# Second attention layer: one 1024-column feature map for two results, sums and evictions issued a product later, query weights cast on POOL

## The chip, the core and the metric

The program runs on one core of one Trainium2 chip. The core has a matrix engine (PE, with its weight loads listed as PEld), a vector engine (DVE), an activation engine (ACT), a general engine (POOL) and DMA queues, here all filled from SP. Each engine works through its own instructions in program order and waits on semaphores for the others. The metric is the device time of one execution in microseconds; lower is better.

## The reference

Four blocks follow each other: attention, feed-forward, attention, feed-forward. Both attention blocks use the same weights, and so do both feed-forward blocks. S is 2048, D is 1024, F is 3584, 32 heads of 32.

```python
phi = lambda t: jnp.where(t > 0, t + 1, jnp.exp(t)) + 1e-6
# attention: q, k, v = layernorm(x) @ wqkv, by heads
pq, pk = phi(q), phi(k)
kv = einsum("bhsd,bhse->bhde", pk, v);  z = sum over s of pk
o = (pq @ kv) / (pq . z + 1e-6);        x = x + o @ wo
# feed-forward: n = layernorm(x)
x = x + ((n @ w_gate) * (n @ w_up)) @ w_down
```

Attention is linear: keys and values of all 2048 rows are first folded into `kv` and `z`, then the queries are run through them.

## The kernel before

`X` holds all 16 row tiles (128 x 1024) on chip. The layers are numbered 0 (attention), 1 (feed-forward), 2 (attention), 3 (feed-forward). The order of work on every engine is the order of the Python calls: loops call a step of matmuls and then whatever small dictionaries (`plan`, filled by `at(step, function, ...)`) have noted for that step. Buffers come from three first-in first-out lists: `banks` (8 PSUM banks of 128 x 512 float32), `temps` (12 tiles of the same size in SBUF) and `slots` (17 tiles of 8 KB per partition). A buffer is put back at the point of the program at which its last use is issued; the next owner waits for that use by semaphore.

Layer 2's keys and values are computed in `kv_seven` (L465) in half precision by a seven-product scheme on 2 x 2 blocks. A group `g` is four row tiles; a unit `u` (8 in all) is one half of it, two row tiles, both for 1024 key columns (k) and 1024 value columns (v). A unit has 14 products of 4 matmuls each (L539), in the order of `SEQ` (L490): "1k 5k 1v 6k 2k 6v 7k 5v 7v 2v 4k 3k 4v 3v". Five PSUM banks carry it: `ak` takes 1k, 6k, 7k, 4k one on top of the other, `av` the same for v, `ck` takes 5k and later 3k, `cv` 5v and 3v, and `b` takes 2k on top of a copy of 1k and then 2v. Because the products pile up in one bank, each intermediate sum is read out between two products: ACT copies (L523, L544), DVE adds (L526). The other three banks hold the running `kv` sums.

Keys go through `phi` (L270): ACT computes an exponential (L277), DVE takes a minimum and adds (L278), DVE adds max(0, x) (L280). This is done four times per unit, for the results of 2k, 7k, 4k and 3k, each 128 x 512. Two of them read PSUM, two read an SBUF tile in which DVE has added two parts. Values are added by DVE straight into `vbs`, and 4v is copied there by ACT (L576). After unit u the matmuls `kp` (L497) fold the two row tiles of unit u-1 into `kv`.

Between the products, `plan` puts other work of the same engines: layernorm of row tiles 8 to 15 (statistics on DVE L220 and L223, inverse deviation on ACT L228 and L229, a small DVE product L231, the normalised tile on ACT L237, a transposing DMA L260), the block differences `x_sum` of the next group (DVE L212), and the cast of the two query weight slots (ACT L177, eight pieces of 128 x 1024). At step 92 both halves of the output weights are loaded.

Ahead of it, `down_seven` (layer 1) has 98 steps of 4 matmuls (L1146), whose own `plan` casts the key and value weights and forms their block sums. Earlier still, in the second pass of layer 1, `scale_begin(2)` and `scale_end(2)` work out the power-of-two scales of the attention weights: `scale_begin` runs ahead of quad 0 and `scale_end` (L359) ahead of quad 1 of that pass (a quad is 56 matmuls on L909). `scale_end` issues transposes on PE (L366), a chain of small DVE instructions (L368 to L383), and in their midst one ACT instruction (L381) that takes the logarithm of the scales `scw` into `lns2`, a bias of the exponentials on L277. ACT's next instructions are the copies of quad 1 (L920).

Of the kernel before, what the change touches and what calls it, by code (L numbers as in the profile page):

```python
# [35 lines left out]
def kernel(  # L36
# [128 lines left out]
    while D % FMAX:  # L165
        FMAX //= 2
    NST = D // FMAX

    ACOL = (1, 0, 2)
    xnTs = {}  # L170
# [4 lines left out]
    def cast_a(m, n, i):  # L175
        s = wA["kqv"[m]][n]
        nc.scalar.activation(out=h3(s, NB)[:, 2 * i:2 * i + 2, :], in_=v3(s, NB)[:, 2 * i:2 * i + 2, :],  # L177
                             func=ACT.Copy, scale=scw[:, 3 + m:4 + m])

    def w_blocks(which):  # L180
        a, b = (h3(s, NB) for s in wA[which])
# [30 lines left out]
        nc.vector.tensor_tensor(out=o, in0=x, in1=y, op=ALU.subtract)  # L212
    lns = {}

    def ln_stats(li, t, parts=tuple(range(NST))):
        if parts[0] == 0:
# [4 lines left out]
        if parts[-1] == NST - 1:  # L221
            mv = lns[(li, t)] = small.tile([P, 2], F32, tag="mv", name="mv")
            nc.vector.bn_aggr(out=mv[:], in_=st[:])  # L223

    def ln_rstd(li, t):
        mv = lns[(li, t)]
# [133 lines left out]
    def scale_end(m):  # L360
        n = NSC[m]
        q, t, qb = qsum.pop(m)
        b = banks.get()
        pt = b[:].bitcast(BF16)[:, 0:3 * P].rearrange("p (m n) -> p m n", n=P)
        for i in range(n):
            nc.tensor.transpose(out=pt[:, i, :], in_=qb[:, i, :], identity=ident[:])  # L366
        temps.put(t)
        nc.vector.tensor_reduce(out=q[:, 0:n], in_=pt[:, 0:n, :], axis=AX.X, op=ALU.add)  # L368
        banks.put(b)
        e = bexp[:, CSC[m]:CSC[m] + n]  # L370
        ei = e.bitcast(I32)
# [6 lines left out]
        nc.vector.tensor_scalar(out=sc, in0=sc, scalar1=AS if m == 2 else WS, scalar2=None, op0=ALU.mult)  # L378
        if m == 2:
            nc.vector.tensor_scalar(out=kaps[:], in0=e, scalar1=1.0 / AS, scalar2=None, op0=ALU.mult)  # L380
            nc.scalar.activation(out=lns2[:], in_=sc[:, 0:2], func=ACT.Ln)  # L381
# [84 lines left out]
    def kv_seven(kvp):  # L466
# [26 lines left out]
        def kp(t, first, last):  # L493
            u = t // TPG * 2 + t % 2
# [9 lines left out]
        def unit(u):  # L504
# [13 lines left out]
            def w4(a):  # L518
                return a[:].rearrange("p (c f) -> p c f", f=P)

            def copy(key, b):
                tm[key] = temps.get()
                nc.scalar.copy(out=tm[key][:], in_=b[:])  # L523

            def add(out, key, b):
                nc.vector.tensor_tensor(out=out, in0=w4(tm[key]) if len(out.shape) == 3 else tm[key][:],  # L526
                                        in1=w4(b) if len(out.shape) == 3 else b[:], op=ALU.add)

            for j, step in enumerate(SEQ.split()):
                i, w = int(step[0]), step[1]  # L530
                key = "b" if i == 2 else ("c" if i in (3, 5) else "a") + w
                if key not in bk:
                    bk[key] = banks.get()
                if i == 1 and w == "k":
                    bk["b"] = banks.get()
                b = bk[key]
                rhs = w_rhs(w, i)
                for k in range(KH):
                    nc.tensor.matmul(out=b[:], lhsT=lhs[i][:, k, pr * P:(pr + 1) * P], rhs=rhs[:, k, :],  # L539
                                     start=k == 0 and (i in (1, 5) or i == 2 and w == "v"), stop=k == KH - 1,  # L540
                                     skip_group_check=True)
                if i == 1:
                    if w == "k":
                        nc.scalar.copy(out=bk["b"][:], in_=b[:])  # L544
                    else:
                        copy("1v", b)
                elif i == 6:
                    copy("6" + w, b)
                elif i == 7:
                    copy("7" + w, b)  # L550
                    if w == "k":
                        add(tm["7k"][:], "7k", bk["ck"])
                        phi(tm["7k"], pk(1, 1), 0)
                    else:
                        add(vb(1, 1), "7v", bk["cv"])
                    temps.put(tm.pop("7" + w))
                elif i == 3:
                    if w == "k":
                        add(tm["6k"][:], "6k", b)
                        phi(tm["6k"], pk(1, 0), 0)  # L560
                    else:
                        add(vb(1, 0), "6v", b)
                    temps.put(tm.pop("6" + w))
                    banks.put(bk.pop(key))
                elif i == 2:
                    if w == "k":
                        phi(b, pk(0, 0), 0)
                    else:
                        add(vb(0, 0), "1v", b)
                        temps.put(tm.pop("1v"))  # L570
                        banks.put(bk.pop("b"))
                elif i == 4:
                    if w == "k":
                        phi(b, pk(0, 1), 0)
                    else:
                        nc.scalar.copy(out=vb(0, 1), in_=w4(b))  # L576
                    banks.put(bk.pop(key))
                for f, args in plan.get(u * 14 + j, ()):
                    f(*args)

        for u in range(2 * NG):
# [4 lines left out]
            if u % 2 == 1:  # L586
                slots.put(xgs.pop(u // 2))

        slots.put(*wA.pop("k"), *wA.pop("v"), wS.pop("k"), wS.pop("v"), wS.pop("d"))

        def rest():
            for t in tiles(2 * NG - 1):
# [446 lines left out]
    def down_seven(q, li, p, hs, wd, load_piece, cast_piece, ORDER, at, run, finish, xrow, nl, W2, final):  # L1039
# [43 lines left out]
        if not final:  # L1083
            if p == 0:
# [156 lines left out]
```

## Time and profile before

| | |
|---|---|
| median of 3 runs | 1521.29 us (1520.68 to 1521.84) |
| profiled execution | 1521.27 us, of which its span 1519.5 us; 1.8 us lie around the span |
| PE | 1495.6 us busy, 98% of the span |
| DVE, ACT, POOL | 987.5, 814.7, 89.6 us busy |
| mean granted PE clock | 0.997 |
| stretch of the 8 units of layer 2 (L539, first to the next stage's first matmul) | 764.98 to 886.03 us |
| PE idle in the span | 24 us |

The trace names stretches of the span by time. Layer 0 lies up to 250 us, layer 1 from 250 to 765 (its second pass from 504), layer 2 from 765 to 1000, layer 3 after it. A wait of PE is shown as the idle time before a matmul and the instruction that ended it; since matmuls overlap by some 0.16 us (379 ns each, one every 216 ns), a gap costs that much more than the idle time shown.

### The profile page before, as it was taken

How to read it: one execution, taken by the hardware profiler on the slowest of the kernel's cores; microseconds unless marked ns; L12 is line 12 of the kernel's file. 1: busy time of each engine (PE TensorE's matmuls, PEld its weight loads, DVE VectorE, ACT ScalarE, POOL GpSimd, SP SyncE). 2: the span in 40 equal slices, each digit the busy share in tenths (PEclk: the TensorE clock that was granted, in tenths of full speed). 3: DMA queues.
4: the chain of work that ended last, by engine and by line, in shares of the span. 5: the costliest groups of instructions: out<-in, count | busy, mean ns of one | idle time of the engine just before them, and what ended most of it. 6: DMA issues, size and time to landing. Idle time of an engine off the chain costs nothing.

```text
span 1519.5 us, 18411 instructions
## 1 busy us (share of the span) xinstructions
PE 1495.6 (98%) x7109; PEld 683.2 (45%) x7109; DVE 987.5 (65%) x1675; ACT 814.7 (54%) x1196; POOL 89.6 (6%) x46
## 2 busy tenths in 40 slices
PE   9999999999999899999997999999999999999999
PEld 4444444444444344444443444444444444444444
DVE  6667989988686566667866676864444853444452
ACT  4678875767667377764447576633334232333420
POOL 0000005971000000000000000000000000000000
PEclk9999999999999999999999999999999999999999
DMA  8696147564489778759421200464223578343513
GB/s 242 181 304 215 56 90 215 149 184 139 129 246 324 222 235 263 242 191 280 147 76 23 75 1 0 146 236 173 111 111 128 159 259 338 120 166 111 196 71 128
DMA packets 219655, 253.90 MB, mean 167 GB/s; under 512 B 68528, under 2 KB 195504, under 8 KB 208816
## 3 DMA queue, kind: packets, MB, share of 16 engines
q1 hardware_dynamic: 219568, 252.74, 52.4%
q8 instruction: 55, 0.90, 0.3%
q14 instruction: 32, 0.26, 0.1%
HBM read 196.08 MB, written 40.89 MB: 156 GB/s over the span
## 4 chain that ended last, share of the span: by engine, by line
PE 92%; DVE 4%; ACT 3%; DMA 1%; issue 0%; SPq 0%; DVEq 0%
PE b L909 44%; PE b L1146 22%; PE b L746 7%; PE b L609 7%; PE b L777 7%; PE b L539 2%; ACT f L277 1%; PE b L760 1%; DVE st L220 1%; DVE s L280 1%; ACT xn L237 1%; DMA s<-in_A_wqkv_dram 1%; PE b L628 0%; DVE f L526 0%; PE b L727 0%; DVE f L278 0%
## 5 line engine op out<-in xcount | busy, mean ns | idle before, releaser
L909 PE MATMUL b<-s,s 128*128 128x512 f16 x3136 | 680.4, 380 | 4.0 <-ACT b L920 4.0
L909 PEld LDWEIGHTS <-s 128*128 128x128 f16 x3136 | 307.1, 98 | 376.2 <-issue 7.6
L1146 PE MATMUL b<-s,s 128*128 128x512 f16 x1568 | 339.1, 379 | 0.0
L925 DVE TENSOR_TENSOR f<-f,b 128x512 f32<-128x512 f32 x232 | 159.3, 687 | 230.6 <-ACT f L914 216.3
L914 ACT COPY f<-b 128x512 f32<-128x512 f32 x284 | 165.9, 584 | 226.8 <-PE b L909 226.8
L1146 PEld LDWEIGHTS <-s 128*128 128x128 f16 x1568 | 153.3, 98 | 185.2
L920 ACT COPY b<-b 128x512 f32<-128x512 f32 x104 | 59.2, 570 | 127.3 <-PE b L909 127.3
L419 ACT ACTIVATE s<-s,scw 128x1024 f16<-128x1024 bf16 x112 | 122.7, 1151 | 2.0 <-DMA s<-in_B_w_gate_dram 1.8
L746 PE MATMUL b<-s,s 128*128 128x512 bf16 (+1 forms) x512 | 120.3, 379 | 0.0
L777 PE MATMUL b<-s,s 128*128 128x512 bf16 x512 | 118.5, 379 | 0.3 <-DVE s L769 0.3
L875 ACT ACTIVATE s<-s,scw 128x1792 f16<-128x1792 bf16 x48 | 83.0, 1783 | 61.6 <-DMA s<-in_B_w_down_dram 54.2
L539 PE MATMUL b<-s,s 128*128 128x512 f16 x448 | 101.6, 379 | 13.8 <-ACT f L523 5.1
L609 PE MATMUL b<-s,s 128*128 128x512 bf16 x512 | 112.1, 379 | 0.9 <-DMA s<-in_A_wqkv_dram 0.7
L830 POOL TENSOR_SCALAR s<-s,scw 128x1024 f16<-128x1024 bf16 x28 | 88.0, 3159 | 257.1 <-DVE X L779 243.9
L929 DVE SCALAR_TENSOR_TENSOR s<-f,b 128x512 f16<-128x512 f32 x108 | 74.2, 687 | 40.8 <-PE b L909 24.4
L929 DVE SCALAR_TENSOR_TENSOR s<-f,f 128x512 f16<-128x512 f32 x116 | 83.2, 717 | 4.0
L220 DVE BATCH_NORM_STATS2 st<-X 128x6 f32<-128x512 bf16 x128 | 82.3, 681 | 2.4 <-DMA X<-in_A_x_dram 2.4
L777 PEld LDWEIGHTS <-s 128*128 128x128 bf16 x512 | 50.0, 98 | 60.9 <-DVE s L769 1.0
L609 PEld LDWEIGHTS <-s 128*128 128x128 bf16 x512 | 49.6, 98 | 60.6 <-issue 1.2
L746 PEld LDWEIGHTS <-s 128*128 128x128 bf16 (+1 forms) x512 | 49.9, 98 | 59.4
L539 PEld LDWEIGHTS <-s 128*128 128x128 f16 x448 | 43.4, 97 | 69.3 <-issue 20.6
L1057 DVE TENSOR_TENSOR s<-s,s 128x1024 f16<-128x1024 f16 x80 | 52.9, 678 | 23.3 <-PE b L1146 23.3
(116 smaller groups left out, 1093.8 us busy)
## 6 DMA issues: line engine op xcount, KB each, us to landing
s<-wc SPq DMA_DIRECT2D x56, 1024.0 KB, 6.6
s<-dc SPq DMA_DIRECT2D x32, 896.0 KB, 5.6
wc<-s SPq DMA_DIRECT2D x28, 1024.0 KB, 5.1
s<-in_B_w_down_dram SPq DMA_DIRECT2D x24, 896.0 KB, 5.7
s<-in_A_wqkv_dram SPq DMA_DIRECT2D x17, 1024.0 KB, 7.9
s<-in_B_w_down_dram SPq DMA_DIRECT2D x14, 1024.0 KB, 7.8
s<-in_B_w_gate_dram SPq DMA_DIRECT2D x28, 512.0 KB, 6.7
s<-in_B_w_up_dram SPq DMA_DIRECT2D x28, 512.0 KB, 7.9
```

Source lines behind the costliest of these rows:

```text
L220: nc.vector.bn_stats(out=st[:, c, :], in_=X[:, t, c * FMAX:(c + 1) * FMAX])
L419: nc.scalar.activation(out=h, in_=v, func=ACT.Copy, scale=scw[:, m:m + 1])
L539: nc.tensor.matmul(out=b[:], lhsT=lhs[i][:, k, pr * P:(pr + 1) * P], rhs=rhs[:, k, :], start=k == 0 and (i in (1, 5) or i == 2 and w == "v ...
L609: nc.tensor.matmul(out=b[:], lhsT=xnT[:, k, tl * P:(tl + 1) * P], rhs=w[:, k, :], start=(k == 0), stop=(k == KD - 1))
L746: nc.tensor.matmul(out=b[:], lhsT=w[:, k, j * P:(j + 1) * P], rhs=xnT[:, k, :], start=(k == 0), stop=(k == KD - 1))
L777: nc.tensor.matmul(out=b[:], lhsT=v3(pqs[g], G)[:, c, tl * P:(tl + 1) * P], rhs=v3(M[n], NB)[:, c, :], start=(c == 0), stop=(c == KD - 1))
L830: nc.gpsimd.tensor_scalar(out=h3(s, D)[:, i, :], in0=v3(s, D)[:, i, :], scalar1=scw[:, 2:3], scalar2=None, op0=ALU.mult)
L909: nc.tensor.matmul(out=o[m][:], lhsT=W.get(j, m, st[i - 1], k), rhs=mv[i - 1][:, k, :], start=start and k == 0, stop=stop and k == KH - 1, ...
L914: nc.scalar.copy(out=d[m][:], in_=o[m][:])
L925: nc.vector.tensor_tensor(out=d[m][:], in0=d[m][:], in1=o[m][:], op=ALU.add)
L929: nc.vector.scalar_tensor_tensor(out=h3(hs[h], 2 * G)[:, pos, g * G:(g + 1) * G], in0=x[:], scalar=HS, in1=y[:], op0=ALU.mult, op1=ALU.mult)
L1146: nc.tensor.matmul(out=bank[(key, tl)][:], lhsT=lhs(i, j, tl), rhs=h3(wd[2 * pi + j // WPC], NB)[:, j % WPC, :], start=(j == 0 and i in (1 ...
```

## The change

The key path of a unit, the order of products, the place of some evictions and several pieces of planned work are different:

- The results of 7k and 3k stay in one 128 x 1024 float32 tile (`wide`, in a slot of its own, one half per unit parity). ACT copies 6k and 7k into its two halves, DVE adds `ck` to each half (`addw`), and one exponential, one minimum/add and one max/add of 1024 columns follow (`phi_exp`, `phi_end`).
- The add of 7k and the two DVE instructions of the wide map are issued one step later, the copy of 4v two steps later, that is after the first product of the next unit. 4k comes before 2v.
- The query weights are cast by POOL (`cast_q`) and loaded at steps 8 and 9. The second half of the output weights is loaded after the last unit.
- Of the layernorm work of tiles 8 to 15, the statistics of the second half of the columns are taken during `down_seven` of layer 1; three tiles use the DVE form of the normalisation (`ln_norm`), and the steps of all are others.
- The logarithm into `lns2` is no longer part of `scale_end`; it is at step 3 of `down_seven`.

```diff
+    def cast_q(n, i):
+        s = wA["q"][n]
+        nc.gpsimd.tensor_scalar(out=h3(s, NB)[:, 2 * i:2 * i + 2, :], in0=v3(s, NB)[:, 2 * i:2 * i + 2, :],
+                                scalar1=scw[:, 4:5], scalar2=None, op0=ALU.mult)
...
+    def last_part(li, t):
+        return 0 if li == 2 and t >= 2 * TPG else NST - 1
+
+    def ln_stats(li, t, parts=tuple(range(NST)), early=False):
+        if early:
+            if not st8:
+                st8.append(temps.get())
...
+    def phi_exp(b, c):
+        m = temps.get()
+        e = m[:].bitcast(BF16)[:, 0:b.shape[-1]]
+        nc.scalar.activation(out=e, in_=b, func=ACT.Exp, bias=lns2[:, c:c + 1], scale=kaps[:, c:c + 1])
+        return m, e
+
+    def phi_end(b, dst, c, m, e):
+        nc.vector.tensor_scalar(out=e, in0=e, scalar1=scw[:, 3 + c:4 + c], scalar2=epss[:, c:c + 1],
+                                op0=ALU.min, op1=ALU.add)
+        nc.vector.scalar_tensor_tensor(out=dst, in0=b, scalar=0.0, in1=e, op0=ALU.max, op1=ALU.add)
+        temps.put(m)
...
-            nc.scalar.activation(out=lns2[:], in_=sc[:, 0:2], func=ACT.Ln)
...
-        for t in range(2 * TPG, NT):
-            i = 4 + 9 * (t - 2 * TPG)
+        for t, i in zip(range(2 * TPG, NT), (3, 8, 17, 31, 36, 45, 59, 64)):
             at(i, ln_stats, 2, t, (0,))
-            at(i + 1, ln_stats, 2, t, (1,))
-            at(i + 3, ln_rstd, 2, t)
-            at(i + 5, ln_apply, 2, t)
-            at(i + 6, tr_tile, 2, t)
-        for g, i in ((1, 15), (2, 46), (3, 76)):
+            if i % 14 == 8:
+                at(i + 5, ln_norm, 2, t)
+                at(i + 6, tr_tile, 2, t)
+            else:
+                at(i + 4, ln_rstd, 2, t)
+                at(i + 6, ln_apply, 2, t)
+                at(i + 7, tr_tile, 2, t)
+        at(66, lambda: temps.put(st8.pop()))
+        for g, i in ((1, 19), (2, 45), (3, 75)):
             for j in range(4):
                 at(i + 2 * j, x_sum, g, j)
-        at(20, load_w, "q", 0)
-        at(21, load_w, "q", 1)
+        at(8, load_w, "q", 0)
+        at(9, load_w, "q", 1)
         for n in range(DC):
             for i in range(4):
-                at(31 + 11 * n + 2 * i, cast_a, 1, n, i)
-        at(92, lambda: wA.update(o=[load_cols(wo_v, n) for n in range(DC)]))
+                at(20 + 16 * n + 4 * i, cast_q, n, i)
+        at(90, lambda: wA.update(o=[load_cols(wo_v, 0)]))
...
-        SEQ = "1k 5k 1v 6k 2k 6v 7k 5v 7v 2v 4k 3k 4v 3v"
+        SEQ = "1k 5k 1v 6k 2k 6v 7k 5v 7v 4k 2v 3k 4v 3v"
+        wides = slots.get()
...
+            def addw(n, b):
+                v = wd2[:, n * NB:(n + 1) * NB]
+                nc.vector.tensor_tensor(out=v, in0=v, in1=b[:], op=ALU.add)
+
+            def out4(b):
+                nc.scalar.copy(out=vb(0, 1), in_=w4(b))
+                banks.put(b)
...
+                elif i in (6, 7) and w == "k":
+                    n = i - 6
+                    nc.scalar.copy(out=wd2[:, n * NB:(n + 1) * NB], in_=b[:])
+                    if i == 7:
+                        later(1, addw, 1, bk["ck"])
...
                 elif i == 3:
                     if w == "k":
-                        add(tm["6k"][:], "6k", b)
-                        phi(tm["6k"], pk(1, 0), 0)
+                        addw(0, b)
+                        later(1, phi_end, wd2, pkv[:, r0 + 1, :], 0, *phi_exp(wd2, 0))
...
                     else:
-                        nc.scalar.copy(out=vb(0, 1), in_=w4(b))
-                    banks.put(bk.pop(key))
-                for f, args in plan.get(u * 14 + j, ()):
+                        later(2, out4, bk.pop(key))
+                for f, args in plan.pop(u * 14 + j, ()):
                     f(*args)
...
+        wA["o"].append(load_cols(wo_v, 1))
...
+                at(3, lambda: nc.scalar.activation(out=lns2[:], in_=scw[:, 3:5], func=ACT.Ln))
+                for u in range(2 * TPG):
+                    at((57, 71)[u // TPG] + 3 * (u % TPG), ln_stats, 2, 2 * TPG + u, (NST - 1,), True)
```

More of the change, by code (lines that the diff above doesn't have):

```diff
@@ L167 @@
     NST = D // FMAX
+    st8 = []
     ACOL = (1, 0, 2)
@@ L213 @@
     lns = {}
-    def ln_stats(li, t, parts=tuple(range(NST))):
-        if parts[0] == 0:
+    def last_part(li, t):
[4 more added lines that the diff above has]
+                st8.append(temps.get())
+            u = 6 * NST * (t - 2 * TPG)
+            lns[(li, t)] = st8[0][:][:, u:u + 6 * NST].rearrange("p (c s) -> p c s", s=6)
+        elif (li, t) not in lns:
             lns[(li, t)] = small.tile([P, NST, 6], F32, tag="st", name="st")
@@ L220, in ln_stats @@
             nc.vector.bn_stats(out=st[:, c, :], in_=X[:, t, c * FMAX:(c + 1) * FMAX])
-        if parts[-1] == NST - 1:
+        if not early and len(parts) == NST or not early and parts[-1] == last_part(li, t):
             mv = lns[(li, t)] = small.tile([P, 2], F32, tag="mv", name="mv")
-            nc.vector.bn_aggr(out=mv[:], in_=st[:])
+            nc.vector.bn_aggr(out=mv[:], in_=st[:] if not isinstance(st, bass.AP) else st)
     def ln_rstd(li, t):
@@ L470, in at @@
             plan.setdefault(step, []).append((f, args))
[L472 to L473 removed]
+        for t, i in zip(range(2 * TPG, NT), (3, 8, 17, 31, 36, 45, 59, 64)):
             at(i, ln_stats, 2, t, (0,))
[L475 to L479 removed]
+            if i % 14 == 8:
[7 more added lines that the diff above has]
+        for g, i in ((1, 19), (2, 45), (3, 75)):
             for j in range(4):
                 at(i + 2 * j, x_sum, g, j)
[L482 to L483 removed]
+        at(8, load_w, "q", 0)
+        at(9, load_w, "q", 1)
         for n in range(DC):
             for i in range(4):
[L486 to L487 removed]
+                at(20 + 16 * n + 4 * i, cast_q, n, i)
+        at(90, lambda: wA.update(o=[load_cols(wo_v, 0)]))
         pks = slots.get()
         pkv = v3(pks, D)
[L491 removed]
+        SEQ = "1k 5k 1v 6k 2k 6v 7k 5v 7v 4k 2v 3k 4v 3v"
+        wides = slots.get()
+        wide = wides[:].bitcast(F32).rearrange("p (u n) -> p u n", n=D)
         def kp(t, first, last):
@@ L519, in w4, with later @@
                 return a[:].rearrange("p (c f) -> p c f", f=P)
+            wd2 = wide[:, u % 2]
+            def later(n, f, *args):
+                at(u * 14 + j + n, f, *args)
             def copy(key, b):
@@ L525, in add @@
             def add(out, key, b):
-                nc.vector.tensor_tensor(out=out, in0=w4(tm[key]) if len(out.shape) == 3 else tm[key][:],
-                                        in1=w4(b) if len(out.shape) == 3 else b[:], op=ALU.add)
+                nc.vector.tensor_tensor(out=out, in0=w4(tm[key]), in1=w4(b), op=ALU.add)
+                temps.put(tm.pop(key))
+            def addw(n, b):
[4 more added lines that the diff above has]
+                banks.put(b)
             for j, step in enumerate(SEQ.split()):
@@ L546, in unit @@
                         copy("1v", b)
+                elif i in (6, 7) and w == "k":
[3 more added lines that the diff above has]
+                        later(1, addw, 1, bk["ck"])
                 elif i == 6:
-                    copy("6" + w, b)
+                    copy("6v", b)
                 elif i == 7:
[L550 to L556, printed above, removed]
+                    copy("7v", b)
+                    add(vb(1, 1), "7v", bk["cv"])
                 elif i == 3:
                     if w == "k":
-                        add(tm["6k"][:], "6k", b)
-                        phi(tm["6k"], pk(1, 0), 0)
+                        addw(0, b)
+                        later(1, phi_end, wd2, pkv[:, r0 + 1, :], 0, *phi_exp(wd2, 0))
                     else:
                         add(vb(1, 0), "6v", b)
-                    temps.put(tm.pop("6" + w))
                     banks.put(bk.pop(key))
@@ L566, in unit @@
                     if w == "k":
-                        phi(b, pk(0, 0), 0)
+                        phi_end(b[:], pk(0, 0), 0, *phi_exp(b[:], 0))
                     else:
                         add(vb(0, 0), "1v", b)
-                        temps.put(tm.pop("1v"))
                         banks.put(bk.pop("b"))
@@ L573, in unit @@
                     if w == "k":
-                        phi(b, pk(0, 1), 0)
-                    else:
-                        nc.scalar.copy(out=vb(0, 1), in_=w4(b))
-                    banks.put(bk.pop(key))
-                for f, args in plan.get(u * 14 + j, ()):
+                        phi_end(b[:], pk(0, 1), 0, *phi_exp(b[:], 0))
+                        banks.put(bk.pop(key))
+                    else:
+                        later(2, out4, bk.pop(key))
+                for f, args in plan.pop(u * 14 + j, ()):
                     f(*args)
@@ L587, in kv_seven @@
                 slots.put(xgs.pop(u // 2))
-        slots.put(*wA.pop("k"), *wA.pop("v"), wS.pop("k"), wS.pop("v"), wS.pop("d"))
+        for i in sorted(plan):
+            for f, args in plan[i]:
+                f(*args)
+        slots.put(*wA.pop("k"), *wA.pop("v"), wS.pop("k"), wS.pop("v"), wS.pop("d"), wides)
+        wA["o"].append(load_cols(wo_v, 1))
         def rest():
```

## The prediction

> **What bounds the kernel now.** First the page: PE is busy 98% of the span, so a gain can only come out of its idle 24 us, or out of time in which it runs slowly. Second the waits of PE, which say where it idles.
>
> ```profile
> PE 1495.6 (98%) x7109; PEld 683.2 (45%) x7109; DVE 987.5 (65%) x1675; ACT 814.7 (54%) x1196; POOL 89.6 (6%) x46
> L539 PE MATMUL b<-s,s 128*128 128x512 f16 x448 | 101.6, 379 | 13.8 <-ACT f L523 5.1 <-DVE f L526 4.6 <-ACT vb L576 1.9
> PE b L539 <- DVE f L526: 4.6, 5, 1.3
> PE b L909 <- ACT b L920: 4.0, 1, 4.0
> ```
>
> Two places hold nearly all of it: the 448 matmuls of the units, with 20 short waits on ACT and DVE, and one wait of 4.0 on L909. The diff touches both, the second by a single moved instruction. Third, the timeline around that wait on PE, ACT and DVE, and the table of stretches beside it:
>
> ```profile
> 516.56 2.75 PE L909 MATMUL b<-s,s 128*128 128x512 f16 x12
> 523.27 8.98 PE L909 MATMUL b<-s,s 128*128 128x512 f16 x29 [3.96 <-ACT b L920]
> 513.62 3.22 ACT L419 ACTIVATE s<-s,scw 128x1024 f16<-128x1024 bf16 x3
> 522.53 0.20 ACT L381 ACTIVATE lns<-scw 128x2 f32<-128x2 f32 x1 [5.69 <-DVE scw L378]
> 522.64 1.06 ACT L920 COPY b<-b 128x512 f32<-128x512 f32 x2
> 522.33 0.17 DVE L378 TENSOR_SCALAR scw<-scw 128x3 f32<-128x3 f32 x1
> ```
>
> ```profile
> 520.00:524.00 4.00, 0.73 (x2) 0.25 (x2) 2.69 (x11) 1.17 (x3) 0.00 (x0) 0.71 0.63 207
> 524.00:526.00 2.00, 2.00 (x6) 0.73 (x5) 0.00 (x0) 0.58 (x1) 0.00 (x0) 0.50 0.84 195
> 526.00:528.00 2.00, 2.00 (x6) 0.67 (x5) 0.00 (x0) 0.58 (x1) 0.00 (x0) 0.50 1.16 328
> ```
>
> ACT is free from 516.84, but its next instruction, the logarithm, waits for the scales until 522.53, and the copies that PE needs stand behind it. In the second fence the PE column says x6 in 2 us at a clock of 0.50, where full speed gives 9: after the gap PE runs at half speed for a while.
>
> Fourth, unit 7 (873.00 to 885.09), which carries no planned work and shows no wait, and last the rows for DVE with POOL busy (250 to 298) and idle (350 to 418):
>
> ```profile
> 883.68 0.41 DVE L278 TENSOR_SCALAR f<-f,scw,epss 128x512 bf16<-128x512 bf16 x1
> 884.73 0.68 DVE L526 TENSOR_TENSOR f<-f,b 128x512 f32<-128x512 f32 x1
> 886.74 0.69 DVE L280 SCALAR_TENSOR_TENSOR s<-f,f 128x512 bf16<-128x512 f32 x1
> 887.35 0.68 DVE L526 TENSOR_TENSOR vb<-f,b 128x512 bf16<-128x512 f32 x1
> ```
>
> ```profile
> L929 DVE SCALAR_TENSOR_TENSOR s<-f,f 128x512 f16<-128x512 f32 x8 | 7.1, 887 | 0.3
> L929 DVE SCALAR_TENSOR_TENSOR s<-f,f 128x512 f16<-128x512 f32 x11 | 7.6, 692 | 0.4
> ```
>
> Two-input SBUF work on DVE stretches by 0.20 per instruction under POOL casts (a half-precision sum, L434, from 0.69 to 0.99 by the same two stretches); what reads PSUM does not (L925 at 0.68 in both).
>
> **The logarithm.** Without it ACT copies as soon as its product is ready. The 12 matmuls from 516.56 end at 519.15 (0.216 each); the first product is ready near 517.4, the copy ends near 518.2, and the matmul that waits could start at 519.15. It started at 523.27: 4.1 us. From there to 528.35, twelve matmuls take 5.08 instead of 2.59: another 2.5. What is late next: the chain on DVE still runs to 522.9, but quad 1's first DVE add has its data only near 523.4; the casts for quad 3 read weights requested at 503.60 and 507.27, landing in 8 us, long before 524. So nothing takes its place: -6.6, bounds -4.1 (slow clock stays for another reason) and -6.6. At step 3 of `down_seven` the same 0.20 waits for nothing, and ACT idles much there (37.8 busy of 85): 0.
>
> The Trainium skill, TensorE: Matmul & The Clock Gate, Part 1 (the HAM clock gate), says that an idle window of about 3.4 us halves the PE clock until a window of work has passed. The rows agree: 4.1 us idle brought 0.50, the units' gaps of up to 1.4 left it at 1.00.
>
> **The units.** They take 886.03 - 764.98 = 121.05. Free of waits it would be 448 x 0.2158 = 96.7 and seven times `kp` at 0.94: 103.3. So 17.8 us are lost (13.8 idle, 0.16 more for each of 20 gaps, the rest in gaps too small to be listed), and no edit here can gain more.
>
> Taken away on ACT: eight casts (L177, 1.14 each, 9.1), and in each unit two exponentials of 0.81 become one of 1024 columns. By the 1024-column L237 that is 1.24. On DVE: half the statistics (8 x 0.69) go to `down_seven`, where DVE has 10.4 of 40 us idle from 725 to 765 and 5.03 in one piece just ahead of the last evictions: 0 there. The wide minimum/add is 0.54 (1024-column L248), the wide max/add 0.69 + 512/0.96 ns = 1.22, an estimate from the per-column slope of the 2048- and 1024-column sums at 1.20 and 0.68. These replace 2 x 0.45 and 2 x 0.61.
>
> So the waits seen now on `ck`, copies and casts should go. The next thing late is a bank. 1v now gets the bank of the last unit's 3v, not that of 4v: with `out4` issued a unit later, the FIFO hands over the 3v bank first. Its last reader is the DVE add of 3v, at the very end of the chain. Worked for a unit without planned work, from its start, with 0.20 from product to reader, 0.04 between DVE and ACT and 0.05 from DVE to PE (all as in unit 7): 4k ends 8.64; exponential 8.84 to 9.62; minimum 9.66, max 10.11; add of 2v 10.72; `addw` of 3k 11.32 to 12.00; wide exponential 12.03 to 13.27; wide minimum 13.31, wide max 13.89 to 15.11; add of 3v 15.03 to 15.71. The next unit's 1v could start after 14 products (12.10), `kp` (0.94) and the two products before it (1.73), at 14.77. PE waits 1.0 us. After unit 0 there is no `kp`: 1.9. Behind it on PE the whole unit waits.
>
> Planned work on the same chain: statistics at step 8 of units 0, 2, 4 push by 0.4; an `x_sum` at step 9 of units 1, 3, 5 by 0.6. That gives 2.3, 1.6, 1.4, 1.6, 1.4, 1.6, 1.0 for the seven hand-overs and 0.5 for the last `kp`, which follows query step 0 and needs the same add: 11.4.
>
> **POOL and the queues.** Eight casts at 3.16 (L830) are 25.3 us on POOL, over two units; the queries need them some 80 us later: 0 by themselves. While they run, four links of the chain (two minima, `x_sum`, the wide max) are SBUF work: 0.2 to 0.3 each, 1.0 per unit, 2.0 in all. Bounds: 0 (nothing lands on the chain) and 2 units x 4 links x 0.83, the largest stretch seen (1.52 for 0.69, at 266.69) = 6.6. I take 2.0, the mean of the rows.
>
> SP: the query loads (7.9 us to landing) stand ahead of the transposing DMAs of tiles 8 to 11, whose readers come 28 us later: 0. The second output load leaves at the last 4v, lands about 6 after the units' end, and is read at 896.27, 10.2 after: 0, or its whole lateness if it took over 12. The transposing DMA of tile 15 lands (3.1) about when unit 5's first `x_sum` asks for it: 0 to 0.5.
>
> Sum: units lose 11.4 + 2.0 = 13.4 instead of 17.8: -4.4, bounds -9.4 (bare hand-overs, 8.4) and +0.2 (18.0 with the largest stretch). With -6.6: -11.0. The profiled execution's 1521.27 (1519.5 span and 1.8 around it; the median is 1521.29) becomes 1510.3.
>
> **Rivals.**
> 1. The hand-over hides better (DVE is ahead of my chain, the stretch misses it): loss 8.4 or less. For: unit 7 had slack everywhere. Against: the chain above is all rows. 1521.3 - 6.6 - 9.4 = 1505.3.
> 2. The units gain nothing: hand-over waits plus POOL eat what casts and statistics gave. For: two of the gaps (2.3 to 3.3) are larger than any now in the units; against: the planned work causes most of today's waits. 1514.7; with one half-clock spell (2.5) 1517.2.
> 3. The logarithm was not what held the copies (another wait shows behind it): 1521.3 - 4.4 = 1516.9. Against: the copies' other waits are over by 514.8.
> 4. Slower: a DVE instruction that meets a POOL cast waits it out. Eight casts could then block DVE for up to 25.3 us in units 0 to 2, nearly all on the chain. It decides once the units lose over 24.4, that is, from 13 us of blocking on top of 11.4. At 20 us of blocking: 1521.3 - 6.6 - 17.8 + 31.4 = 1528.3. Against: in 250 to 298 POOL cast without a break and the means are 0.89 and 0.99 for 0.69, with PE never waiting. The Trainium skill, SBUF — State Buffer, "SBUF: two separate sides", states this rule: the shared port pair is held for the whole instruction and the loser fully blocks. The means do not bear it out in that size.
>
> **How the numbers follow.** Forecast (1508 to 1513) 0.50; rival 1 0.22, rival 2 0.18, rival 3 0.05, rival 4 0.03, others 0.02. The range takes in rival 1 below and most of rival 2 above: 1504 to 1516. A change under 0.2% (3.0 us) can't be told from none here. Slower by more is rival 4 (0.03); within 0.2% part of rivals 2 and 3 with another loss (0.03); faster 0.94.
>
> **What would show it.** The wait on L909 behind L920 and the clock of 0.50 near 524 are gone. In the units PE's waits are seven, nearly all at 1v on the DVE add of a value bank, the first two the longest, with about 11 to 12 us idle; no waits on the copies of 6k, 7k, 6v, 7v. The wide max shows near 1.22. POOL shows 36 casts. The prediction is wrong if PE waits elsewhere in the units, if a gap there brings the half clock, or if the copies of quad 1 still come late.

## The result and the profile after

The changed kernel takes 1509.47 us (median of 6 runs, 1508.08 to 1510.73) against 1520.5 for the kernel before, measured beside it (6 runs, 1519.78 to 1521.84). The ratio is 0.9927, with an interval of 0.9914 to 0.9939. The forecast was 1510.3 in a range of 1504 to 1516. The profiled execution took 1509.88, of which 1508.1 is its span.

The page first: the line of busy times, and the row of the units' matmuls (now L582).

```profile
PE 1490.2 (99%) x7075; PEld 683.7 (45%) x7109; DVE 987.1 (65%) x1659; ACT 803.8 (53%) x1177; POOL 112.3 (7%) x54
L582 PE MATMUL b<-s,s 128*128 128x512 f16 x448 | 100.7, 383 | 10.1 <-DVE vb L561 10.1
```

Next the waits of PE. The columns are the total, the number of waits and the longest.

```profile
PE b L582 <- DVE vb L561: 10.1, 7, 2.5
PE b L527 <- DVE vb L561: 0.4, 1, 0.4
```

The five kinds of wait in the units (on three kinds of ACT copies and two of DVE adds, 20 in all) have become one kind, with seven. All seven are on the DVE add into a value tile. The second row is the same add, late for the last `kp`, behind the units. The wait of 4.0 behind ACT's copies in layer 1 is not listed any more. The timeline of PE and ACT at the place where it stood, and the stretches beside it (length, then busy time of PE, PEld, DVE, ACT and POOL, then the granted clock):

```profile
516.13 14.19 PE L954 MATMUL b<-s,s 128*128 128x512 f16 x65
...
517.20 0.57 ACT L965 COPY b<-b 128x512 f32<-128x512 f32 x1 [0.78 <-PE b L954]
518.06 0.57 ACT L965 COPY b<-b 128x512 f32<-128x512 f32 x1 [0.29 <-PE b L954]
```

```profile
520.00:524.00 4.00, 4.00 (x20) 1.86 (x19) 3.09 (x12) 2.31 (x5) 0.00 (x0) 1.00 0.71 213
524.00:526.00 2.00, 2.00 (x11) 0.89 (x10) 1.34 (x3) 2.00 (x4) 0.00 (x0) 1.00 0.91 231
```

Quad 1 runs through in one piece, its copies wait for nothing but their own product, and the clock stays at 1.00 where it was 0.50.

Now the units. These are the end of unit 4 on DVE and the start of unit 5's `1v` on PE, from two timelines:

```profile
831.64 0.55 DVE L291 TENSOR_SCALAR f<-f,scw,epss 128x1024 bf16<-128x1024 bf16 x1 [1.31 <-ACT f L287]
832.23 1.23 DVE L293 SCALAR_TENSOR_TENSOR s<-s,f 128x1024 bf16<-128x1024 f32 x1
833.37 0.68 DVE L561 TENSOR_TENSOR vb<-f,b 128x512 bf16<-128x512 f32 x1
...
831.04 1.89 PE L582 MATMUL b<-s,s 128*128 128x512 f16 x8
834.11 2.10 PE L582 MATMUL b<-s,s 128*128 128x512 f16 x9 [1.17 <-DVE vb L561]
```

DVE works off the wide minimum and the wide max/add, then the add of 3v, and 0.06 after that add PE starts again. One place is new, behind the longest of the seven waits, after unit 0 (the same columns of stretches):

```profile
774.00:776.00 2.00, 1.52 (x4) 0.56 (x4) 1.99 (x3) 0.00 (x0) 2.00 (x2) 0.56 0.00 0
776.00:778.00 2.00, 2.00 (x7) 0.73 (x6) 0.21 (x1) 0.63 (x2) 2.00 (x2) 0.58 0.69 131
778.00:780.00 2.00, 2.00 (x11) 0.93 (x10) 0.36 (x1) 1.64 (x3) 2.00 (x2) 1.00 0.00 0
```

PE stood for 2.48 and then ran at about half its clock for some 3 us: its next 48 matmuls took 12.07, where 48 take 10.52 in the units after, so 1.55 were lost. Such a stretch at half clock behind a gap is called a slow spell below.

Between the two traces the time went as follows. The units now start at 757.87 instead of 764.98, 7.11 earlier; 0.43 of that was already there when quad 0 started, and 6.68 comes from the stretch with the logarithm. The units take 116.18 (757.87 to 874.05) instead of 121.05, 4.87 less. What follows them is 0.58 longer, of which 0.52 is the wait at the last `kp`. The sum is 11.4, the difference of the spans.

### The profile page after: what moved, and what is told of

Read it like the earlier page. It is cut to its first block, busy times and chain, and to the rows that moved or that the text cites. A ratio compares the mean times of both kernels' runs of the same rounds, so it can differ in the third digit from the quotient of the medians.

```text
span 1508.1 us, 18371 instructions
## 1 busy us (share of the span) xinstructions
PE 1490.2 (99%) x7075; PEld 683.7 (45%) x7109; DVE 987.1 (65%) x1659; ACT 803.8 (53%) x1177; POOL 112.3 (7%) x54
## 4 chain that ended last, share of the span: by engine, by line
PE 94%; DVE 4%; ACT 1%; DMA 1%; issue 1%; SPq 0%; DVEq 0%
PE b L954 45%; PE b L1194 22%; PE b L791 7%; PE b L654 7%; PE b L822 7%; PE b L582 4%; ACT f L287 1%; PE b L805 1%; DVE vb L561 1%; DVE s L293 1%; DVE f L291 1%; DMA s<-in_A_wqkv_dram 1%; PE b L673 1%; PE b L772 0%; DVE s L566 0%
## 5 line engine op out<-in xcount | busy, mean ns | idle before, releaser
L582 PE MATMUL b<-s,s 128*128 128x512 f16 x448 | 100.7, 383 | 10.1 <-DVE vb L561 10.1
L234 DVE BATCH_NORM_STATS2 st<-X 128x6 f32<-128x512 bf16 x112 | 71.7, 681 | 2.2 <-DMA X<-in_A_x_dram 2.2
L582 PEld LDWEIGHTS <-s 128*128 128x128 f16 x448 | 43.9, 99 | 64.0 <-issue 14.4
```

## The experiments

**The logarithm alone.** The kernel before, with only the move of the one ACT instruction:

```diff
-            nc.scalar.activation(out=lns2[:], in_=sc[:, 0:2], func=ACT.Ln)
...
+                at(3, lambda: nc.scalar.activation(out=lns2[:], in_=scw[:, 3:5], func=ACT.Ln))
```

> The kernel before with one edit: the logarithm into lns2 is taken out of scale_end and issued at step 3 of down_seven. Theory (ACT waited for the scales and held PE, then PE ran at half clock): the wait on the copy ahead of quad 1 and the 0.50 clock behind it are gone, 6.6 us less than before (4.1 idle and 2.5 slow), the units unchanged at 121. Rival (the copies would have come late anyway, or the slow clock has another cause): 0 to 4.1 less.

Measured: 1514.45 (1514.44 to 1514.47) against 1521.19 for the kernel before, ratio 0.9956 (0.9941 to 0.9971). The gap and the slow spell are gone, and the units' waits are those of before (5.1, 4.6, 1.9, 1.7 and 0.4 us by kind). So one instruction of 0.20 us was worth 6.7.

**The logarithm put back.** The changed kernel with that move alone undone (the same diff, reversed).

> The changed kernel with the logarithm put back into scale_end. Theory: 6.6 us more than the changed kernel, so about 4.5 less than before, the units still at 116.2. If the two parts of the change help each other, the loss against the changed kernel is another one than what the logarithm alone gains.

Measured: 1514.71 (1514.15 to 1516.34), ratio 0.996 (0.9946 to 0.9975), 5.2 above the changed kernel. The wait of 4.0 behind ACT's copies is back. Its timeline of PE, in layer 1 and after unit 0, and the stretches in layer 1:

```profile
523.73 6.52 PE L955 MATMUL b<-s,s 128*128 128x512 f16 x23 [3.96 <-ACT b L966]
...
780.98 10.52 PE L583 MATMUL b<-s,s 128*128 128x512 f16 x48 [2.59 <-DVE vb L562]
```

```profile
524.00:526.00 2.00, 2.00 (x6) 0.73 (x5) 0.00 (x0) 0.53 (x2) 0.00 (x0) 0.50 0.98 203
526.00:528.00 2.00, 2.00 (x10) 0.81 (x8) 0.00 (x0) 0.80 (x2) 0.00 (x0) 0.86 1.09 318
```

The gap has its old size. Two things make the sum smaller than 6.6. The slow spell is shorter: 23 matmuls took 6.52 where 22 x 0.216 + 0.38 = 5.13 would do, so 1.4 instead of 2.5. And the wait of 2.59 after unit 0 brought no slow spell here, which is worth 1.5 (units 114.68 instead of 116.18). With 0.9 of a later start-up: 0.9 + 4.1 + 1.4 - 1.5 = 4.9, and the spans differ by 4.8. The same wait thus halves the clock in one execution and not in another.

**The wide map behind the add of 3v.** The two DVE instructions of the wide map are issued one step later, so that they stand behind the add of 3v; nothing is left out.

```diff
-                        later(1, phi_end, wd2, pkv[:, r0 + 1, :], 0, *phi_exp(wd2, 0))
+                        later(2, phi_end, wd2, pkv[:, r0 + 1, :], 0, *phi_exp(wd2, 0))
```

> The changed kernel with one number changed: the two DVE instructions of the wide map are issued two steps later instead of one, so they stand behind the DVE add of 3v. Theory (the only thing that PE waits for in the units is the bank of 3v, whose reader stands behind the wide map): all seven waits at 1v and the one of the last kp go, 11.7 us less than the changed kernel, about 1498, the units near 104.5. Rival (DVE and ACT are full, the next wait is right behind): waits of 4 us or more stay, on ck or on the copy of 4v, 1502 or more.

Measured: 1497.02 (1496.72 to 1498.85), ratio 0.9844 (0.983 to 0.9859). The row of the units' matmuls in its groups, and two pieces of its timeline:

```profile
L582 PE MATMUL b<-s,s 128*128 128x512 f16 x448 | 98.1, 379 | 0.0
```

```profile
758.08 24.62 PE L582 MATMUL b<-s,s 128*128 128x512 f16 x112
...
861.66 1.89 PE L791 MATMUL b<-s,s 128*128 128x512 f16 x8
```

PE waits for nothing in the units; they take 103.58, against the 103.3 that the forecast worked out as free of waits, and 12.6 less than in the changed kernel. The same instructions are 12.5 us cheaper in this order.

**Another bank.** DVE keeps its order, and the copy of 4v is issued one step later instead of two; its bank then goes to the next `1v`, and that of 3v to a later product.

```diff
                         later(1, phi_end, wd2, pkv[:, r0 + 1, :], 0, *phi_exp(wd2, 0))
+                        banks.put(bk.pop(key))
                     else:
                         add(vb(1, 0), "6v", b)
-                    banks.put(bk.pop(key))
+                        later(1, banks.put, bk.pop(key))
...
-                        later(2, out4, bk.pop(key))
+                        later(1, out4, bk.pop(key))
```

> The changed kernel with the order of two bank returns changed: the copy of 4v is issued one step later instead of two, the bank of 3v is put back behind it, so that 1v gets the bank of 4v. DVE's order is that of the changed kernel. Theory (the hand-over of the 3v bank, not DVE time as such): the waits at 1v go except up to 0.4 after unit 0, the 0.5 at the last kp stays, 10.8 less than the changed kernel, about 1499. Rival (DVE is late whatever bank is handed over): 5v or another product waits instead, less than half of the 11.7 is gained.

Measured: 1498.81 (1498.07 to 1500.17), ratio 0.9854 (0.984 to 0.9869). Of the units' waits one of 0.69 is left, after unit 0, on ACT. The end of unit 4 on DVE and the start of unit 5 on PE, from its timelines:

```profile
825.66 1.23 DVE L293 SCALAR_TENSOR_TENSOR s<-s,f 128x1024 bf16<-128x1024 f32 x1
826.80 0.68 DVE L561 TENSOR_TENSOR vb<-f,b 128x512 bf16<-128x512 f32 x1
...
823.54 1.11 PE L527 MATMUL b<-vb,s 128*128 128x129 bf16 x16
824.48 5.77 PE L582 MATMUL b<-s,s 128*128 128x512 f16 x26
```

The add of 3v ends 3.9 after `kp` starts, and so it does in the changed kernel (unit 4: `kp` at 830.10, the add's end at 834.05). So the chain is no shorter, but PE runs on past it: `1v`, eight matmuls after 824.48, starts near 826.2 while the add is not even begun. The length of the chain alone costs nothing. It takes both, the bank of 3v handed to `1v` and the wide map ahead of that bank's last reader: the run before took the second away, this one the first.

**Two maps.** The changed kernel, with the map of 7k issued as soon as its sum stands, and the map of 3k alone behind 3k.

```diff
-                        later(1, addw, 1, bk["ck"])
+                        def half(b5=bk["ck"]):
+                            addw(1, b5)
+                            h = wd2[:, NB:D]
+                            later(1, phi_end, h, pk(1, 1), 0, *phi_exp(h, 0))
+                        later(1, half)
...
-                        later(1, phi_end, wd2, pkv[:, r0 + 1, :], 0, *phi_exp(wd2, 0))
+                        later(1, phi_end, wd2[:, 0:NB], pk(1, 0), 0, *phi_exp(wd2[:, 0:NB], 0))
```

> The changed kernel with the 1024-column map split into two maps of 512 again: the half of 7k is mapped as soon as its sum stands, the half of 3k as before, one step after 3k; everything else stays. Theory (the add of 3v stands behind the wide map, and the next unit's 1v waits for its bank): behind the sum of 3k the chain is one exponential of 0.78 instead of 1.24, a minimum of 0.41 instead of 0.55 and a max/add of 0.69 instead of 1.23, so the add of 3v ends 1.1 us earlier in each unit. Of the waits of the changed kernel (2.64, 1.69, 1.33, 1.59, 1.33, 1.59, 0.99 with the overlap of 0.16 each, and 0.52 at the last kp) 1.5, 0.6, 0.2, 0.5, 0.2, 0.5 and 0 stay, 3.5 in all: 8 us less than the changed kernel, 1501.5 (1500 to 1504), though ACT then works some 0.3 us and DVE some 0.3 us more per unit. Rival (the wide map itself brings the gain, by less ACT and DVE work): the waits stay or grow, 1509.5 or more, up to 1514.

Measured: 1515.84 (1514.4 to 1517.49), ratio 0.997 (0.9959 to 0.9982): a miss by 14 us, and on the other side of the changed kernel. The rival, that the waits stay or grow, had the direction. The waits of PE in this run, and DVE at the end of unit 5 from its timeline:

```profile
PE b L582 <- DVE vb L561: 11.0, 7, 2.3
PE b L582 <- DVE s L566: 2.2, 6, 0.7
PE b L582 <- DVE s L293: 1.7, 1, 1.7
```

```profile
848.25 0.69 DVE L561 TENSOR_TENSOR vb<-f,b 128x512 bf16<-128x512 f32 x1 [1.35 <-ACT f L558]
848.86 0.41 DVE L291 TENSOR_SCALAR f<-f,scw,epss 128x512 bf16<-128x512 bf16 x1
849.30 0.69 DVE L293 SCALAR_TENSOR_TENSOR s<-s,f 128x512 bf16<-128x512 f32 x1
...
852.16 0.68 DVE L566 TENSOR_TENSOR s<-s,b 128x512 f32<-128x512 f32 x1
...
854.77 0.68 DVE L561 TENSOR_TENSOR vb<-f,b 128x512 bf16<-128x512 f32 x1
```

The expectation took the map of 7k off the chain. But DVE has no pause there: from the add of 7v at 848.25 to the sum of 3k (852.16 + 0.68) it works back to back, so the map of 7k (1.1) pushes that sum back. And the exponential of 7k on ACT holds up the copy of 7v, so the add of 7v starts 1.35 after DVE had become free. The add of 3v gains nothing, and the sum of 3k, whose bank the next unit's `5k` takes, becomes a second thing to wait for. The units take 122.47 (758.23 to 880.70), more than the 121.05 of the kernel before: with this hand-over of banks, nothing of the units' gain is left without the one wide map.

**POOL kept busy.** The changed kernel, with three more casts in place by 1.0 behind each query cast.

```diff
+    def again_q(n, i):
+        v = h3(wA["q"][n], NB)[:, 2 * i:2 * i + 2, :]
+        nc.gpsimd.tensor_scalar(out=v, in0=v, scalar1=1.0, scalar2=None, op0=ALU.mult)
...
+                for r in range(3):
+                    at(21 + 16 * n + 4 * i, again_q, n, i)
```

> The changed kernel, with each of the eight casts of the query weights on POOL followed by three more of the same size in place by 1.0, which change no value: POOL is then busy from about 760 to about 850, over seven units instead of two. Theory (a POOL instruction stretches a DVE one now and then, by a few tenths on the chain, as in unit 0, where the wide minimum took 0.85 for 0.55): 0 to 0.6 per unit in the five units that are new under it, 1.5 us more than the changed kernel, 1511.0 (1509.5 to 1513). Rival (a DVE instruction that meets a POOL cast waits for the rest of that cast, up to 2.8 us): in five units with four SBUF links each on the chain, at half a cast for each, 5 x 4 x 1.4 = 28 us more; even at one meeting per unit 7 us more, 1516.5 or more.

Measured: 1520.94 (1509.75 to 1521.82), ratio 0.9986 (0.9964 to 1.0008). Seven of ten executions lie above 1520 and three below 1512; the three have a mean clock of 0.999 to 1.000, the seven of 0.994. The profiled one took 1521.74. Its seven waits are 14.3 in all, the longest 2.8. DVE at the end of unit 4 and PE in the unit after it, from its timelines:

```profile
840.68 0.92 DVE L295 TENSOR_SCALAR f<-f,scw,epss 128x1024 bf16<-128x1024 bf16 x1 [1.31 <-ACT f L291]
841.64 2.01 DVE L297 SCALAR_TENSOR_TENSOR s<-s,f 128x1024 bf16<-128x1024 f32 x1
...
844.31 12.21 PE L588 MATMUL b<-s,s 128*128 128x512 f16 x48 [2.33 <-DVE vb L567]
```

Neither expectation held: the three short executions lie in the theory's range and the seven long ones above the rival's 1516.5, but not for the rival's reason. Beside the casts the wide minimum took 0.92 for 0.55 and the wide max/add 2.01 for 1.23, so this wait grew from 1.17 to 2.33; over the units the waits grew by 4.2, not by 1.5. And five of the seven waits are now 2.1 or more, and behind each of the five the 48 matmuls take 12.2 instead of 10.52. These slow spells are 8.4 against 1.55 in the changed kernel. Together 4.2 + 6.9 = 11.1, of 11.9 between the spans; the other 0.8 is a later start of the units. In this execution the stretch makes the gaps longer, and the clock behind them makes the larger part of the price. Without its spells it would have taken 1513.3, and the three shorter ones lie 1.5 to 3.6 below that, so a part of the longer waits was absent there too. Why, the runs do not show: none of the three shorter ones left a trace.

**The casts on ACT.** The changed kernel with the query casts on ACT, at the same steps.

```diff
-                at(20 + 16 * n + 4 * i, cast_q, n, i)
+                at(20 + 16 * n + 4 * i, cast_a, 1, n, i)
```

> The changed kernel with the eight casts of the query weights on ACT again, at the same steps (20, 24, ... 48); all else stays. Theory (the hand-over of the 3v bank sets the waits, not ACT's load): the stretch of 0.3 in unit 0 goes; of the eight casts of 1.14 only that at step 8 of unit 2 stands right ahead of a link of the chain, the exponential of 4k, and makes it up to 0.9 late: 1510.1 (1509 to 1511.5), with the longer wait after unit 2. Rival (the casts on ACT were what held PE in the units before, and their move to POOL is where the units' gain came from): waits on ACT copies come back, 4 us or more, 1513.5 or more.

Measured: 1510.53 (1509.66 to 1511.35), ratio 0.9937 (0.9922 to 0.9952). The seven waits are 10.5 in all: 0.37 less after unit 0, 0.21 to 0.31 more after units 1 to 3. The time is as expected, but a single longer wait, after unit 2, had been. So where the casts run is worth about 1 us here, within a run's scatter, and the casts on ACT were not what held PE.

**The statistics in the units.** The changed kernel with the second half of the statistics one step behind the first instead of in layer 1.

```diff
-        return 0 if li == 2 and t >= 2 * TPG else NST - 1
+        return NST - 1
...
+            at(i + 1, ln_stats, 2, t, (1,))
...
-        at(66, lambda: temps.put(st8.pop()))
...
-                for u in range(2 * TPG):
-                    at((57, 71)[u // TPG] + 3 * (u % TPG), ln_stats, 2, 2 * TPG + u, (NST - 1,), True)
```

> The changed kernel with the second half of the statistics of tiles 8 to 15 back in the units, one step behind the first half, instead of during layer 1; all else stays. Theory: a further 0.69 on DVE ahead of the wide map counts only in the units whose first half lies at step 8 (0, 2 and 4): the waits after these grow by 0.6 each, 1.8 in all, 1511.3 (1510.5 to 1512); the waits after units 1, 3, 5 and 6 stay. Rival (DVE has room for it everywhere): 1509.5. Second rival (DVE is the bound in all units, each further us on it counts): 8 x 0.69 = 5.5 more, 1515.

Measured: 1512.88 (1511.2 to 1515.57), ratio 0.9954 (0.9939 to 0.9969), 3.4 above the changed kernel. The waits after units 2 and 4 grew by 0.69 each, those after 1, 5 and 6 by at most 0.1 downwards, as expected. Not expected: 0.25 more after unit 3; after unit 0 only 0.21 more, but a second wait of 0.68 beside it and a longer slow spell (2.8 for 1.55). So of the 3.4 some 1.3 are clock, not DVE time.

**The new order without the moves.** The wide map behind the add of 3v, with casts on ACT and statistics in the units (the three diffs above together).

> The wide map issued behind the add of 3v, as in the run that took the hand-over out, and two of the moves of the change undone with it: the casts of the query weights on ACT again, the second half of the statistics in the units again. Theory (these moves only shortened a wait that this order does not have; the add of 3v has 1.7 us in hand there): 1497 (1496 to 1499), no wait of PE on the add of 3v. Rival (the moves carry weight of their own, as the 3.4 us that the statistics cost the changed kernel): 1500 to 1502.

Measured: 1499.26 (1498.67 to 1500.17), ratio 0.9861 (0.9846 to 0.9876), between the two expectations. No wait is left on the add of 3v, but three others: 0.29 and 0.92 on ACT's copy of 1k (at the longer one a cast of 1.13 stands ahead of it, at the shorter one none), and 0.23 on a sum. So the new order without these two moves is 10.2 below the changed kernel, and 12.5 with them: the moves are worth 2.2 in it.

**The new order with POOL busy.** The wide map behind the add of 3v, with POOL's additional casts.

> The wide map issued behind the add of 3v, and POOL kept busy through seven units by three more casts in place behind each query cast, as before. Theory (the kernel with POOL kept busy lost 4.2 us by longer waits, because the wide minimum took 0.92 for 0.55 and the wide max/add 2.02 for 1.23 ahead of the add of 3v, and the rest, some 7 us, by five spells at half clock behind gaps of 2.3 us and more): here the stretched instructions stand behind the add, there is no gap and so no spell: 1497.5 (1496.5 to 1499). Rival (DVE, busy some 80% of a unit, runs out of time once POOL stretches it by 1 to 1.5 us per unit): waits of 0.5 to 1 us in five units, 1500 to 1503 without a spell.

Measured: 1497.93 (1497.5 to 1498.05), ratio 0.9851 (0.9836 to 0.9866). DVE is still stretched (the `x_sum` instructions, 0.69, have means of 0.91 and 0.93, the wide minimum 0.75), and PE waits for nothing in the units, as expected. The wide max/add takes 1.23 here throughout, though POOL is as busy. The same work on POOL that cost 11.5 us costs 0.9 here.

**The new order with two maps.** The wide map split as in the run above, the second half behind the add of 3v.

> The wide map split in two maps of 512, the second of them issued behind the add of 3v. Theory (with two maps DVE works back to back from the add of 7v on, the first map is in the way of the sum of 3k, and the next unit's 5k waits for that sum's bank, 0.2 to 0.7 each in the run with two maps): six such waits of 0.2 to 0.7 stay, with the overlap 3.2 us more than the one wide map in this order, 1500.2 (1498.5 to 1503). Rival (in this order the width of the map does not matter): 1497.

Measured: 1504.04 (1503.04 to 1505.12), ratio 0.9891 (0.9875 to 0.9908), 7 above the one wide map in this order, where 3.2 had been expected. The row of the waits that the expectation had, and of the one that it lacked:

```profile
PE b L582 <- DVE s L566: 2.3, 6, 0.8
PE b L582 <- DVE s L293: 2.0, 1, 2.0
```

The six waits for the sum of 3k are there. The seventh is after unit 0: the max/add of 4k stands behind the map of 7k, and the next unit's `1k` wants its bank. The minima of these two maps took 0.83 and 1.09 there, beside POOL's casts, for 0.41 elsewhere, so 1.1 of this wait is POOL's stretch. Three short waits, 0.7 in all, are left on other copies and adds. So the one wide map, in a place where nothing waits behind it, is worth 7 us against this split, about 1 of them through the casts.

## Why the prediction was right, point by point

**The logarithm: -6.6.** Right, in size and mechanism. Alone it gave 6.7, in the trace of the changed kernel 6.68, and put back it brought the wait of 4.0 and the clock of 0.50. The half-clock part is not a constant: 2.5 in the trace of before, 1.4 in that of the logarithm put back. Of the 31 executions of the kernel before that stand beside the experiments, 13 have a mean clock of 0.997, like the profiled one, and 18 one of 0.998 or 0.999. They average 1521.3 and 1520.2, and the difference of 1.1 is that of 2.5 and 1.4. So the 2.5 was probably the longer of two lengths; only one execution was traced.

**What is late next in the units: 11.4 for the hand-over of the 3v bank.** Right in mechanism and size, with one price that its rows do not give. Forecast were 2.3, 1.6, 1.4, 1.6, 1.4, 1.6, 1.0 and 0.5 at the last `kp`. The trace has, with 0.16 for each gap, 2.64, 1.69, 1.33, 1.59, 1.33, 1.59, 0.99 and 0.52, in all 11.7. That it is the bank, and which instructions stand ahead of its last reader, is shown by the two runs that took each away: 1498.81 and 1497.02. The chain worked out by hand from single rows came out because DVE takes its instructions in the order of the program and their durations repeat where POOL is not in the way (wide max/add 1.22 estimated, 1.23 measured; minimum 0.54 and 0.55; exponential 1.24 and 1.24). But the 1.22 does not follow from the two sums named as its source: they differ by 0.52 for 1024 columns, so 512 more columns would be 0.26, the max/add 0.95 and each of the eight hand-overs 0.27 shorter, 9.2 in all. The 512/0.96 ns that was used instead, about 1.04 ns a column, is what the new instruction then showed.

**POOL's stretch: 2.0.** The step that was mis-sized. In the changed kernel's trace the casts run from 759.86 to 782.48. These are the two minima that they stretched most, from DVE's timeline:

```profile
771.72 0.85 DVE L291 TENSOR_SCALAR f<-f,scw,epss 128x1024 bf16<-128x1024 bf16 x1 [1.31 <-ACT f L287]
779.64 1.26 DVE L291 TENSOR_SCALAR f<-f,scw,epss 128x512 bf16<-128x512 bf16 x1 [3.40 <-ACT f L287]
```

The first took 0.85 for 0.55; it is the wide minimum of unit 0, on the chain: 0.3. The second took 1.26 for 0.41; it is early in unit 1, and the wait after that unit is only 0.10 longer than those after units 3 and 5, which have the same planned work. So the stretch cost about 0.4, and without it the waits are 11.3. The casts took 2.85 each instead of 3.16; the rows of POOL by groups, with the casts of layer 1's down weights, from which the forecast took its price, and those of the query weights:

```profile
L875 POOL TENSOR_SCALAR s<-s,scw 128x1024 f16<-128x1024 bf16 x28 | 88.0, 3160 | 256.8 <-DVE X L824 243.5 <-PE b L954 10.8 <-DMA s<-in_B_w_down_dram 2.4
L183 POOL TENSOR_SCALAR s<-s,scw 128x1024 f16<-128x1024 bf16 x8 | 22.6, 2846 | 412.6 <-DMA s<-in_A_wqkv_dram 412.6
```

The forecast used a mean over rows, but what a chain meets depends on when it meets it: the run with POOL kept busy shows 1.16 in one unit.

**The clock in the units: nothing.** Wrong by 1.55 in the profiled execution. The forecast's own list of what would make it wrong had a gap that brings the half clock, and the gap of 2.48 after unit 0 did. The units lost 12.9 (116.18 - 103.3) and 0.5 falls after them, 13.4 as forecast, but by two errors that cancel: the waits, with their stretch, are 11.7 and the spell 1.55. That the sum came out is luck. Of the six executions two, the profiled one among them, have a mean clock of 0.999 and average 1510.3, and four have 1.000 and average 1509.1; so most of them probably had no such spell, but none of these was traced.

**The casts at nothing, and the statistics.** The query weights came in time, and POOL shows 36 casts. The statistics were costed at 0 in layer 1, which the start of the units bears out, and their removal was not costed by itself; it is worth 3.4 in the changed kernel.

**The rivals.** The hand-over did not hide better (7 waits, as worked out). The units gained 4.87, so rival 2 falls. Rival 3 falls with the logarithm alone. Rival 4, DVE blocked by the casts, does not show in this kernel. The run made to provoke it did come out slow, but with 4.2 of longer waits, where its price had been 28, and 6.9 of slow clock.

**Not taken apart.** The change also puts 4k ahead of 2v, issues the add of 7k a step later and moves the layernorm steps. No run undoes these alone, so what each of them carries is not shown.

## What to carry to other kernels

Buffers from a first-in first-out list tie the next stage to whichever instruction read the buffer last: before splitting or speeding up the work in a chain, look at what stands ahead of that reader on its engine, and move it behind (12.5 us here, by one digit). A small instruction on an in-order engine that waits for another engine costs what stands behind it, so put it where its input is long ready. When a wait grows past some 2 us, price the slow clock behind it with the wait, as something that can come or stay away.

## What the runs showed of the hardware

The clock was halved by shorter gaps than thought. The forecast had 4.1 as enough and 1.4 as too little. Gaps of 2.1 to 2.8 us of listed idle time brought a clock of 0.50 in the changed kernel, with the casts on ACT, with the statistics in the units, and five times with POOL kept busy; a gap of 2.59 did not, with the logarithm put back, nor one of 2.32 in the run with two maps. In the same run one of 1.60 did once, with 0.72 of idle time and four matmuls ahead of it, and four others of 1.60, with 0.17 to 0.63 ahead, did not. The spells cost 1.5 to 2.8. The Trainium skill, TensorE: Matmul & The Clock Gate, Part 1 (the HAM clock gate), has the clock fall after an idle window of about 3.4 us, in a window that runs freely. That the same gap halves the clock in one execution and not in another would fit a window that runs freely; that the window must be idle throughout does not, since these gaps are all shorter than it.

A DVE instruction beside POOL casts was stretched by up to 0.85 us (a minimum of 1.26 for 0.41 in the changed kernel, a wide max/add of 2.01 for 1.23 with POOL kept busy), while one cast takes some 2.84. The Trainium skill, SBUF — State Buffer, "SBUF: two separate sides", has the later one blocked until the other's instruction ends, where the DVE instruction has two SBUF inputs or runs in a 2-port mode. The runs show no delay of more than 0.9 us in one instruction, and many none: in the new order with POOL busy every wide max/add beside the casts, with two SBUF inputs, took 1.22 or 1.23.
